# Attention for one query per head: the second halving moved to the last two quarters of a tile, and the norms read behind the third product

## The chip, the core and the metric

The kernel runs on one core of a Trainium2 chip. The metric is the device time of one execution in microseconds, lower is better. A ratio is the mean time of one kernel's fast runs over the mean of the other's fast runs in the same rounds, so it is not quite the ratio of the medians that are quoted. A difference counts as faster or slower when it is clear of 2% ("class" in the table of the experiments). Where two runs that differ by less are still called faster or slower than each other, the ranges of their single times don't overlap.

PE is the matrix engine, VectorE (DVE), ScalarE (ACT) and SyncE (SP) are the others used here; SP's queue issues the loads, ScalarE's the outputs. K(t) and V(t) are the loads of the keys and values of tile t. The norm is the sum by which an output is divided. A hole is a stretch in which fewer than half of the 16 DMA engines are at work.

## The reference

Eight batches of 32 heads, one query per head, 4096 keys and values of 128 numbers, all bf16:

```python
B, H, Sq, Skv, Dh = 8, 32, 1, 4096, 128
scale = q.shape[-1] ** -0.5
scores = jnp.einsum('bhqd,bhkd->bhqk', q, k) * scale
attn = _softmax(scores, axis=-1)
return jnp.einsum('bhqk,bhkd->bhqd', attn, v)
```

Each K and V is used once, so 537 MB have to come in and next to nothing goes out.

## The kernel before

The 256 heads go in 32 tiles of 8. A tile of K and a tile of V are 8.389 MB each (64 KB on each of 128 partitions), and three such buffers go round for both. For each tile, VectorE multiplies K by q quarter by quarter and halves the 128 products of a key to 64 (and in some quarters to 32); PE adds these up in groups with an identity matrix, 8 matmuls for 64 columns, 4 for 32; VectorE reduces what PE leaves.

```python
def width_of(t, u):
    return D // 4 if u < NU // 2 and t < NT - 3 else D // 2

def product(t, lo, hi):            # one quarter
    ...                            # tensor_tensor kt * qb, then first halving to D/2
    if width_of(t, c0 // UC) < D // 2:
        nc.vector.tensor_tensor(...)      # second halving to D/4

def sum_over_d(t, u):
    n = width_of(t, u) // DS              # DS = 8: 8 matmuls, or 4
    for s in range(n):
        nc.tensor.matmul(ps[:], lhsT=ident[:], rhs=kt[...], ...)
```

The values are multiplied in a loop on PE, one tile behind. The loop is a critical section (a block with a branch into it, which PE alone runs), and loads are kept behind it in program order:

```python
def values_loop(t):
    ...
    with tc.tile_critical() as loop:
        ...                                # 2 matmuls, 10 iterations of 6, 2 matmuls
    loops.append(loop)
```

Every two tiles, a norm is ready, and every eight tiles a finished block of 16 KB is sent out by ScalarE's queue:

```python
def finish_of(n):
    s, u = divmod(n, OB)                   # OB = 4
    ...
    nc.scalar.activation(out=stages[s][:, u, :], in_=ops.pop(n)[:], func=ACT.Copy, scale=rzs.pop(n)[:, 0:1])
    ...
    if u == OB - 1 or ...:
        nc.scalar.dma_start(o_n[s, ...], stages[s][...])

for t in range(NT):
    ...
    product(t, 0, Q)
    sum_over_d(t, 0)
    if t > 2 and t % R == 1:
        recip_of(n)
        finish_of(n)
    if t + 1 < NT:
        q_prep(t + 1)
    product(t, Q, 2 * Q)
    sum_over_d(t, 1)
    scores_of(t, 0)
    product(t, 2 * Q, 3 * Q)
    sum_over_d(t, 2)
    scores_of(t, 1)
    product(t, 3 * Q, C)
    sum_over_d(t, 3)
    scores_of(t, 2)
    if loop:
        values_loop(t - 1)
        load("k", t + 1)
        load("v", t)
    ...
```

## Time and profile before

| | before |
|---|---|
| time, median (lowest to highest) | 1300.55 us (1299.94 to 1301.36) |
| span of the profiled run | 1297.3 us |
| V issues apart, odd and even tiles, mean | 43.3 and 37.2 us |
| holes in the load stream | one of 5.1 us, 14 of 1.0 to 2.8 us |

Two groups of the page matter. A line gives the source line, the engine, the operation with its tiles and shapes, then busy time and mean, then the idle time ahead of these instructions and what ended most of it:

```profile
L217 DVE TENSOR_REDUCE sc<-ps 128x64 f32<-128x512 f32 x128 | 87.9, 687 | 116.2 <-PE ps L205 116.2
...
L336 DVE RECIPROCAL rz<-zp 16x1 f32<-16x1 f32 x16 | 2.5, 155 | 70.0 <-PE zp L328 70.0
```

VectorE (DVE) waits 116 us in all for PE's sums, most of it once at each tile's end, and 70 us, 4.7 on average in 15 odd tiles, for a norm that PE makes behind its loop.

### The profile page before, as it was taken

The numbers are of one execution on the slowest core, as the hardware profiler recorded it, in microseconds if no ns is written. First come the engines' busy times: TensorE is split into PE (matmuls) and PEld (weight loads), VectorE is DVE, ScalarE is ACT, GpSimd is POOL, SyncE is SP. The second block draws the span as 40 slices with busy tenths as digits, with TensorE's granted clock in tenths as the row PEclk, the third lists the DMA queues.
The fourth block names the chain that finished last, engine by engine and source line by source line (L and its number), as shares of the span: only waits on it lengthen the run. The fifth ranks groups of instructions, "written<-read, shape, count | busy, mean of one in ns | idle before, by whom it ended". The sixth has DMA issues, their size and how long they took to land. (4 is left out here: it accounts for less than half of the span.)

```text
span 1297.3 us, 11039 instructions
## 1 busy us (share of the span) xinstructions
PE 814.7 (63%) x3067; PEld 293.8 (23%) x3067; DVE 1040.1 (80%) x588; ACT 172.3 (13%) x625; POOL 3.3 (0%) x18
## 2 busy tenths in 40 slices
PE   1266576665776646776466764667646676567855
PEld 0022122221222212222122221222212222122212
DVE  5887886877969779687796878978788787887784
ACT  0111011110111101111011110111111111101111
POOL 0000000000000000000000000000000000000000
PEclk9998688786888868878688777887768887688867
DMA  9989999999999999999999999999999999999997
GB/s 422 420 356 443 429 390 451 390 420 421 420 421 409 430 390 421 451 390 421 421 420 421 396 445 388 436 437 386 422 388 451 423 388 451 390 420 434 403 451 300
DMA packets 11433, 537.33 MB, mean 414 GB/s; under 512 B 1808, under 2 KB 2064, under 8 KB 2320
## 3 DMA queue, kind: packets, MB, share of 16 engines
q1 hardware_dynamic: 11072, 536.94, 96.6%
q8 instruction: 14, 0.23, 0.1%
q10 hardware_dynamic: 336, 0.07, 0.0%
q14 instruction: 11, 0.09, 0.0%
HBM read 536.94 MB, written 0.07 MB: 414 GB/s over the span
## 5 line engine op out<-in xcount | busy, mean ns | idle before, releaser
L185 DVE TENSOR_TENSOR kt<-kt,qb 128x8192 bf16<-128x8192 bf16 x128 | 565.2, 4416 | 50.2 <-DMA kt<-in_k_dram 33.9
L205 PE MATMUL ps<-kt,ident 128*128 128x512 bf16 x792 | 316.0, 563 | 397.6 <-DVE kt L188 301.6
L288 PE MATMUL av<-vt,w 128*32 x1740 | 423.1, 382 | 9.8
L188 DVE TENSOR_TENSOR kt<-kt 128x4096 bf16<-128x4096 bf16 x128 | 293.4, 2292 | 4.4
L205 PEld LDWEIGHTS <-ident 128*128 128x128 bf16 x792 | 98.9, 129 | 596.9 <-issue 579.5
L288 PEld LDWEIGHTS av<-vt,w 128*32 x1740 | 165.4, 95 | 270.2 <-issue 146.3
L249 ACT ACTIVATE w<-sc,bias 128x256 bf16<-128x256 f32 x256 | 126.4, 494 | 711.1 <-DVE bias L240 711.1
L217 DVE TENSOR_REDUCE sc<-ps 128x64 f32<-128x512 f32 x128 | 87.9, 687 | 116.2 <-PE ps L205 116.2
L193 DVE TENSOR_TENSOR kt<-kt 128x2048 bf16<-128x2048 bf16 x58 | 71.0, 1225 | 2.0
L344 ACT ACTIVATE comb<-av 32x512 bf16<-32x512 f32 (+1 forms) x32 | 18.7, 586 | 322.7 <-PEq L278 316.7
L336 DVE RECIPROCAL rz<-zp 16x1 f32<-16x1 f32 x16 | 2.5, 155 | 70.0 <-PE zp L328 70.0
L274 PE MATMUL av<-vt,w 128*32 128x512 bf16 x116 | 42.0, 450 | 14.3 <-issue 12.7
L249 ACT ACTIVATION_READ_ACCUMULATOR w<-sc,bias 128x1 f32 x256 | 47.7, 186 | 0.0
L360 PE MATMUL op<-comb,pick 32*16 32x128 bf16 (+1 forms) x128 | 12.1, 213 | 25.6 <-ACT comb L344 25.6
L274 PEld LDWEIGHTS av<-vt,w 128*32 128x32 bf16 x116 | 6.8, 99 | 54.0 <-issue 54.0
L168 ACT ACTIVATE qg<-qh 8x128 bf16<-8x128 f32 x32 | 8.5, 266 | 69.1 <-PE qh L164 63.0
L170 PE MATMUL qp<-qg,heads 8*128 8x128 bf16 x32 | 7.0, 217 | 16.7 <-ACT qg L168 16.7
L360 PEld LDWEIGHTS <-pick 32*16 32x16 bf16 (+1 forms) x128 | 8.8, 83 | 32.7 <-issue 32.2
L164 PE MATMUL qh<-q_all,ident 128*8 128x128 bf16 x32 | 7.2, 224 | 13.1 <-DMA q_all<-in_q_dram 13.1
L229 DVE TENSOR_REDUCE pmax<-sc 128x1 f32<-128x256 f32 x32 | 13.4, 420 | 1.1
L316 PE MATMUL av<-vt,w 128*32 128x512 bf16 x191 | 14.0, 402 | 0.0
L172 ACT ACTIVATE qb<-qp 128x128 bf16<-128x128 f32 x32 | 8.9, 277 | 9.7 <-PE qp L170 9.7
(29 smaller groups left out, 50.7 us busy)
## 6 DMA issues: line engine op xcount, KB each, us to landing
kt<-in_k_dram SPq DMA_DIRECT2D x7, 4096.0 KB, 21.1
kt<-in_k_dram SPq DMA_DIRECT2D x2, 2048.0 KB, 14.0
vt<-in_v_dram SPq DMA_DIRECT2D x1, 4096.0 KB, 30.4
vt<-in_v_dram SPq DMA_DIRECT2D x1, 2048.0 KB, 34.9
vt<-in_v_dram SPq DMA_DIRECT2D x1, 1024.0 KB, 36.9
vt<-in_v_dram SPq DMA_DIRECT2D x1, 512.0 KB, 37.6
vt<-in_v_dram SPq DMA_DIRECT2D x31, 23.9
kt<-in_k_dram SPq DMA_DIRECT2D x28, 26.5
```

Of the source, the lines that this page charges most:

```text
L185: nc.vector.tensor_tensor(out=part, in0=part, in1=qb[:].to_broadcast([P, MC, D]), op=ALU.mult)
L188: nc.vector.tensor_tensor(out=part[:, :, 0 : D // 2], in0=part[:, :, 0 : D // 2], in1=part[:, :, D // 2 : D], op=ALU.add,)
L193: nc.vector.tensor_tensor(out=part[:, :, 0 : D // 4], in0=part[:, :, 0 : D // 4], in1=part[:, :, D // 4 : D // 2], op=ALU.add,)
L205: nc.tensor.matmul(ps[:], lhsT=ident[:], rhs=kt[:, u * UC : (u + 1) * UC, s * DS : (s + 1) * DS], start=(s == 0), stop=(s == n - 1),)
L217: made = nc.vector.tensor_reduce(out=scs[t][:, u * UC : (u + 1) * UC], in_=sums.pop((t, u))[:], axis=AX.X, op=ALU.add)
L229: nc.vector.tensor_reduce(out=pmax[:], in_=sc[:], axis=AX.X, op=ALU.max)
L249: nc.scalar.activation(out=w[:, :, g, :], in_=sc_g, func=ACT.Exp, bias=bias[:, g : g + 1], scale=scale, accum_out=esum[:, t % R, g : g + 1],)
L274: pe.matmul(av, lhsT=wf[:, i * nw : (i + 1) * nw], rhs=vf[:, i * nv : (i + 1) * nv], **how)
L288: pe.matmul(av, lhsT=wf[:, bass.ds(ow + i * nw, nw)], rhs=vf[:, bass.ds(ov + i * nv, nv)], start=False, stop=False,)
L316: nc.tensor.matmul(avs[t][j * AG : (j + 1) * AG, :], lhsT=w[:, i, :, :], rhs=vt[:, c0 : c0 + CB, :], start=(i < TG), stop=(j not in group[ ...
L344: nc.scalar.activation(out=comb[0:n, :, :], in_=av[0:n, :, :], func=ACT.Copy)
L360: nc.tensor.matmul(ops[n][:], lhsT=pick[0:e, m, r, :], rhs=comb[0:e, m, :], start=(r == 0 and m == 0), stop=(r == R - 1 and m == CB - 1),)
```

## The change

Its intent is to shorten what stands between the landing of a K tile and the release of its buffer. Four sums instead of eight remain at the end of a tile, and VectorE no longer stops for the norm in the middle of it.

```diff
-        return D // 4 if u < NU // 2 and t < NT - 3 else D // 2
+        return D // 4 if u >= NU // 2 and t < NT - 3 else D // 2
@@ the loop over tiles
             product(t, 0, Q)
             sum_over_d(t, 0)
-            if t > 2 and t % R == 1:
-                recip_of(n)
-                finish_of(n)
             if t + 1 < NT:
                 q_prep(t + 1)
             product(t, Q, 2 * Q)
@@
             sum_over_d(t, 2)
             scores_of(t, 1)
+            if t > 2 and t % R == 1:
+                recip_of(n)
+                finish_of(n)
             product(t, 3 * Q, C)
```

## The prediction

> **What bounds the kernel now.** I first read the page for the whole, then the queue that issues the loads, then a table of four tiles, then the timeline of the two VectorE stretches between them.
>
> ```profile
> DMA  9989999999999999999999999999999999999997
> q1 hardware_dynamic: 11072, 536.94, 96.6%
> HBM read 536.94 MB, written 0.07 MB: 414 GB/s over the span
> ```
>
> The kernel streams 537 MB and the DMA engines look full. But 414 GB/s is a mean over the span; what matters is what the stream does when nothing holds it. The table of stretches (length, then busy times by engine, granted clock, DMA share, GB/s) says it:
>
> ```profile
> 645.90:647.70 1.80, 1.37 (x5) 0.17 (x3) 0.96 (x2) 0.00 (x0) 0.00 (x0) 0.62 0.44 146
> 655.00:720.00 65.00, 41.09 (x151) 14.79 (x151) 53.15 (x29) 6.66 (x23) 0.00 (x0) 0.78 1.01 435
> ```
>
> Undisturbed it moves 435 GB/s, a load of 8.389 MB in 19.3 us; at 646 there is a hole. From the packets' starts and ends I counted such holes (fewer than half of the 16 engines at work): one of 5.1 us at 80, then 14, one every second tile (163.8, 243.5, 324.0 ... 1209.4), 1.0 to 2.8 us each and 30 us together. The issuing queue shows why:
>
> ```profile
> 603.34 0.33 SPq L151 DMA_DIRECT2D vt<-in_v_dram  x1
> 620.21 0.33 SPq L151 DMA_DIRECT2D kt<-in_k_dram  x1
> 646.70 0.33 SPq L151 DMA_DIRECT2D vt<-in_v_dram  x1
> 663.52 0.33 SPq L151 DMA_DIRECT2D kt<-in_k_dram  x1
> 683.87 0.33 SPq L151 DMA_DIRECT2D vt<-in_v_dram  x1
> 700.80 0.33 SPq L151 DMA_DIRECT2D kt<-in_k_dram  x1
> 727.29 0.33 SPq L151 DMA_DIRECT2D vt<-in_v_dram  x1
> ```
>
> Three buffers of a whole tile go round, so V(t) may be loaded when the last sum over K(t) on PE has ended, and K(t+2) when the loop over V(t-1) has (16.8 us after). V issues are 43.4 and 37.2 us apart in turn, 80.5 a pair. In the short (even) tile VectorE never waits for data. In the long (odd) one it waits for K, and the queue, already empty, waits for it:
>
> ```profile
> 609.16 4.42 DVE L185 TENSOR_TENSOR kt<-kt,qb 128x8192 bf16<-128x8192 bf16 x1 [3.88 <-DMA kt<-in_k_dram]
> ...
> 620.47 0.16 DVE L336 RECIPROCAL rz<-zp 16x1 f32<-16x1 f32 x1 [3.29 <-PE zp L328]
> ...
> 646.71 0.69 DVE L217 TENSOR_REDUCE sc<-ps 128x64 f32<-128x512 f32 x1 [3.06 <-PE ps L205]
> ```
>
> K lands at 609.2, V is issued at 646.7: 37.5 us, plus about 1 us to the first packet, while the two loads queued behind K take 2 x 19.3 = 38.6 us plus their own start. The hole is that chain, and 3.3 us of it is VectorE waiting for a norm behind the loop on PE, 3.1 us the eight last sums.
>
> **What the Trainium skill says.** "DMA: Bandwidth & Descriptors", Where 436 GB/s comes from: a fabric ceiling of 435.2 GB/s. The 435 above agrees, so the stream can't get faster; only holes can be closed. "TensorE: Matmul & The Clock Gate", Part 1: with 512 columns matmuls start 426.7 ns apart on a cold array and 215.7 ns warm, in windows of about 3.4 us. The trace agrees: eight sums take 3.57 us cold, 1.90 us right after the loop. So where the eight stand matters. "VectorE: DVE Perf Modes", Side-by-side: 2048 bf16 results of a tensor_tensor in 2x mode take about 1224 ns; the second halving measures 1225. "Perfetto Trace Analysis", Optimization Strategy: a gap that repeats on the engine that should be saturated can mean too few buffers; here it is the three.
>
> **The change part by part.** No instruction is added or removed: 58 second halvings and 792 sum matmuls remain, they change places. Rows used:
>
> ```profile
> 628.58 1.86 PE L205 MATMUL ps<-kt,ident 128*128 128x512 bf16 x4 [5.60 <-DVE kt L193]
> 643.10 3.57 PE L205 MATMUL ps<-kt,ident 128*128 128x512 bf16 x8 [3.69 <-DVE kt L188]
> 664.53 1.04 PE L205 MATMUL ps<-kt,ident 128*128 128x512 bf16 x4
> 1227.24 1.90 PE L205 MATMUL ps<-kt,ident 128*128 128x512 bf16 x8
> 1229.18 0.69 DVE L217 TENSOR_REDUCE sc<-ps 128x64 f32<-128x512 f32 x1 [4.49 <-PE ps L205]
> ```
>
> (a) The last quarter has 4 sums, not 8: cold, 3.57 becomes 1.86. V is issued 1.71 us sooner in every tile up to 28.
> (b) The first quarter has 8 warm sums behind the loop: 1.04 becomes 1.90, +0.86.
> (c) Each of the last two quarters has a second halving on VectorE, +1.27 each (from the first halving to the next instruction 2.21 becomes 2.33 + 1.15); each of the first two has 1.27 less.
> (d) The reciprocal no longer stands between the first two quarters. Its norm is finished by the third, so it costs about 0.1 and waits for nothing.
>
> Two recurrences result. *From K's landing* (if K is late): 2 x 6.7 for the first two quarters, then 0.60 + 4.45 + 2.33 + 1.15 = 8.53 each for the last two, 0.13 to PE, 1.86 of sums: 13.4 + 17.1 + 2.0 = 32.5 us, against 37.5 now. That is 5 us sooner, more than the 2.2 us hole. *From V issue to V issue over PE*: loop, copy, output sums, first quarter's 8 sums, their reduction. Tile 30 of the kernel before, which has no second halvings, already has this form: V issue 1209.39, reduction at 1229.18, so 19.8 us. Then 2 x 8.53 + 0.13 + 1.86 + 0.03: 38.9 us. Before it was 18.9 + 2 x 7.26 + 0.13 + 3.57 = 37.2, as seen. So the even tile gets 1.7 us *longer* and the odd one falls to the same 38.9. VectorE reaches its first reduction about 15.4 us after V issue, PE 19.8, so VectorE now waits there some 4.4 us in every tile. And K may land some 4 us late without harm.
>
> The DMA needs 38.6 us per tile. One engine of the 16 falls about 1.2 us behind whenever one of the 14 instruction packets of 16 KB (page part 3, queue q8, about one in 98 us) comes by; at worst, always on the same engine, this adds 0.5 a tile: 38.6 to 39.1. So both limits lie at 38.9 to 39.1, against 80.5 / 2 = 40.2. I take 39.1 for steps that don't always mesh.
>
> The sum: tiles 0 and 1 are VectorE's, without a loop in front, and lose 1.71 each: V(1) at 84.3 - 3.4 = 80.9 (a hole of about 1.7 us stays there). 27 tiles of 39.1 bring V(28) to 1136.6. Tile 29 (no second halvings, before and after) takes about 38.3: V(29) at 1174.9, before 1209.4. From there to the end, 87.9 us, nothing changes. That is 34.5 us less. 1300.6 - 34.5 = 1266; for waits I haven't seen I add 2: **1268 us, 2.5% less**.
>
> **Rivals.** *1. The PE chain becomes longer than I say.* The loop used to begin behind eight sums that had nearly warmed the array; now it begins 1.7 us sooner in the clock's window and runs its first 1 to 4 us cold. For: cold matmuls come 427 ns apart, while the loop issues one in 251. Against: loops that began up to 2.0 us before the clock rose (tile at 969.5) still ended 16.86 us after V issue, against 16.82 for others, because six warm matmuls need 1.3 us of the 1.5 us an iteration takes, and the queue catches up. If it costs 0.6 us a tile, 16 us of the gain go: 1284. *2. DMA was full anyway* (96.6%), so only bits come back. For: the page. Against: the holes, 35 us in all, and 435 GB/s between them. If half of the holes reopen elsewhere (K late, the slow engine lagging ever further): 1284 as well. *3. Only the odd tile matters and the even one keeps 37.2.* Then DMA's 38.6 sets the pace and no more: 1254 to 1258. Against: the wait of 4.49 us at 1229.18, which shows the even tile can't. *4. Slower*: would need over 41 us a tile; nothing shows that.
>
> **Range and chances.** Every 0.1 us per tile is 2.7 us in the end. 38.85 gives about 1260, 39.5 about 1277. Two per cent less is 1274.6, or 39.4 us per tile: above my estimate of either limit, but only by 0.3. So faster by over 2% 0.74, within 2% 0.25, slower 0.01; range 1261 to 1278.
>
> **What would show it right or wrong.** Right: V issues about 39 us apart without alternation; the holes at every second tile gone and a mean of some 425 GB/s; no wait of VectorE for the norm; a wait of 4 to 5 us for the first quarter's sums in every tile up to 28; the wait at the tile's end near 1.4 us instead of 3.1; VectorE's waits for K short or gone. Wrong: an interval from V to K well above 17 us (rival 1); V issues even but 39.5 or more apart with VectorE waiting for K (rival 2); alternation still there.

## The result

| | before | after |
|---|---|---|
| time, median (lowest to highest) | 1300.55 us (1299.94 to 1301.36) | 1280.87 us (1280.28 to 1282.37) |
| ratio, 95% interval | | 0.985, 0.9833 to 0.9867: the same at 2% |
| span of the profiled run | 1297.3 us | 1280.6 us |

The kernel is 1.5% faster. The prediction was 1268 us with a range up to 1278, and faster by over 2% at 0.74. The measured time lies 13 us above the one and 3 us above the other.

The load stream of the changed kernel, from its page:

```profile
q1 hardware_dynamic: 11072, 536.94, 98.0%
HBM read 536.94 MB, written 0.07 MB: 419 GB/s over the span
```

It is fuller than the 96.6% and 414 GB/s of before, but below the 425 GB/s that the prediction named as the sign of success. In one tile of it, VectorE's timeline (start, duration, line, operation, and in brackets the idle time before and what ended it) is mostly as foretold:

```profile
616.99 0.69 DVE L217 TENSOR_REDUCE sc<-ps 128x64 f32<-128x512 f32 x1 [2.07 <-PE ps L205]
...
626.12 0.15 DVE L336 RECIPROCAL rz<-zp 16x1 f32<-16x1 f32 x1
...
636.13 0.69 DVE L217 TENSOR_REDUCE sc<-ps 128x64 f32<-128x512 f32 x1 [1.35 <-PE ps L205]
...
640.20 4.42 DVE L185 TENSOR_TENSOR kt<-kt,qb 128x8192 bf16<-128x8192 bf16 x1 [2.14 <-DMA kt<-in_k_dram]
```

The reciprocal waits for nothing, the wait at the tile's end is 1.35 us instead of 3.06, there is a new wait for the first quarter's sums, and K is waited for in odd and even tiles alike. What was not foretold is in the queue that issues the loads:

```profile
353.62 0.33 SPq L151 DMA_DIRECT2D vt<-in_v_dram  x1
370.44 0.33 SPq L151 DMA_DIRECT2D kt<-in_k_dram  x1
392.53 0.33 SPq L151 DMA_DIRECT2D vt<-in_v_dram  x1
419.36 0.33 SPq L151 DMA_DIRECT2D kt<-in_k_dram  x1
441.32 0.33 SPq L151 DMA_DIRECT2D vt<-in_v_dram  x1
```

As a rule V issues are 38.9 us apart, and K follows V after 16.8 us. But here K follows after 26.8 and the next V after 48.8. Of the 28 intervals from V(1) to V(29) three are like that: 48.8, 43.7 and 44.4 us. Against 38.9 these are 20.2 us too much in all. They belong to tiles 9, 17 and 25. The timeline of PE and of ScalarE's queue in tile 9 shows what happened:

```profile
383.10 7.00 ACTq L375 DMA_DIRECT2D out_dram<-stage  x1
...
390.63 1.86 PE L205 MATMUL ps<-kt,ident 128*128 128x512 bf16 x4 [6.71 <-DVE kt L193]
...
402.75 1.03 PE L274 MATMUL av<-vt,w 128*32 128x512 bf16 x2 [10.25 <-DMA out_dram<-stage]
```

The last sums end at 392.5. The loop over the values (L274 is its first line) should begin 0.4 us later, and it begins 10.2 us later, when an output transfer has landed. The load stream then runs dry. This is the view of stretches of the changed kernel, in the order length, busy times, granted clock, DMA share, GB/s:

```profile
415.00:420.30 5.30, 4.40 (x22) 1.64 (x20) 0.00 (x0) 0.59 (x1) 0.00 (x0) 1.00 0.00 0
```

In the kernel before, the same transfer of the same tile was issued at 380.54, and its loop was not late:

```profile
380.54 5.98 ACTq L375 DMA_DIRECT2D out_dram<-stage  x1
...
405.82 0.61 PE L274 MATMUL av<-vt,w 128*32 128x512 bf16 x2 [0.55 <-issue]
```

There the transfer had 25 us until the loop; now it has 10. The last packets of the three outputs end at 401.6, 718.1 and 1035.3 in the changed kernel, and the three late loops begin at 402.75, 719.04 and 1036.06, 0.8 to 1.2 us later each time:

```profile
719.04 1.04 PE L274 MATMUL av<-vt,w 128*32 128x512 bf16 x2 [5.06 <-DMA kt<-in_k_dram]
...
1036.06 1.03 PE L274 MATMUL av<-vt,w 128*32 128x512 bf16 x2 [5.54 <-DMA out_dram<-stage]
```

(For the second the profile names a load of K as the releaser; that load landed at 718.78, the output at 718.58, so the label alone decides nothing. In both_send_loop below, the same loop begins at 704.44, well before that K, on which VectorE starts at 709.86.)

### The profile page after: what moved, and what is told of

Read it like the earlier page. It is cut to its first block, busy times and chain, and to the rows that moved or that the text cites. A ratio compares the mean times of both kernels' runs of the same rounds, so it can differ in the third digit from the quotient of the medians.

```text
span 1280.6 us, 11028 instructions
## 1 busy us (share of the span) xinstructions
PE 766.2 (60%) x3067; PEld 287.8 (22%) x3067; DVE 1040.6 (81%) x588; ACT 172.4 (13%) x625; POOL 3.3 (0%) x18
## 5 line engine op out<-in xcount | busy, mean ns | idle before, releaser
L185 DVE TENSOR_TENSOR kt<-kt,qb 128x8192 bf16<-128x8192 bf16 x128 | 565.2, 4416 | 70.0 <-DMA kt<-in_k_dram 58.5
L205 PE MATMUL ps<-kt,ident 128*128 128x512 bf16 x792 | 261.0, 480 | 419.9 <-DVE kt L193 369.7
L288 PEld LDWEIGHTS av<-vt,w 128*32 x1740 | 173.0, 99 | 263.9 <-issue 123.2
L205 PEld LDWEIGHTS <-ident 128*128 128x128 bf16 x792 | 84.5, 113 | 571.2 <-issue 523.2
L274 PE MATMUL av<-vt,w 128*32 128x512 bf16 x116 | 47.3, 501 | 34.0 <-DMA out_dram<-stage 15.8
L274 PEld LDWEIGHTS av<-vt,w 128*32 128x32 bf16 x116 | 7.1, 101 | 74.1 <-issue 73.7
L369 ACT ACTIVATE stage<-op,rz 16x128 bf16<-16x128 f32 x16 | 5.7, 358 | 132.4 <-DVE rz L336 132.0
L316 PE MATMUL av<-vt,w 128*32 128x512 bf16 x191 | 15.4, 418 | 0.0
## 6 DMA issues: line engine op xcount, KB each, us to landing
vt<-in_v_dram SPq DMA_DIRECT2D x1, 1024.0 KB, 38.7
```

The costliest lines, as they stand in the source:

```text
L185: nc.vector.tensor_tensor(out=part, in0=part, in1=qb[:].to_broadcast([P, MC, D]), op=ALU.mult)
L205: nc.tensor.matmul(ps[:], lhsT=ident[:], rhs=kt[:, u * UC : (u + 1) * UC, s * DS : (s + 1) * DS], start=(s == 0), stop=(s == n - 1),)
L274: pe.matmul(av, lhsT=wf[:, i * nw : (i + 1) * nw], rhs=vf[:, i * nv : (i + 1) * nv], **how)
L288: pe.matmul(av, lhsT=wf[:, bass.ds(ow + i * nw, nw)], rhs=vf[:, bass.ds(ov + i * nv, nv)], start=False, stop=False,)
L316: nc.tensor.matmul(avs[t][j * AG : (j + 1) * AG, :], lhsT=w[:, i, :, :], rhs=vt[:, c0 : c0 + CB, :], start=(i < TG), stop=(j not in group[ ...
```

## The experiments

Theory A: the loop's entry waits for every transfer issued ahead of it, so the moved output stalls it three times, and that is where the missing gain went. Theory B: the load stream was full anyway, or the stalls have another cause that only coincides with the output. Beside it stood the question which of the two parts carries the gain. Eleven kernels ran, three rounds each; all gave correct results.

| run | median us | median before | ratio | 95% interval | class |
|---|---|---|---|---|---|
| both_send_behind | 1281.81 | 1299.55 | 0.9855 | 0.9839 to 0.9872 | same |
| widths_only | 1316.61 | 1299.55 | 1.0132 | 1.0115 to 1.0149 | same |
| norms_only | 1276.19 | 1299.55 | 0.9815 | 0.9799 to 0.9832 | unclear |
| norms_send_behind | 1275.20 | 1299.55 | 0.981 | 0.9794 to 0.9827 | unclear |
| both_send_loop | 1260.92 | 1299.74 | 0.9701 | 0.9685 to 0.9717 | faster |
| norms_send_loop | 1264.34 | 1299.74 | 0.9724 | 0.9708 to 0.974 | faster |
| norms_second | 1265.50 | 1299.74 | 0.9726 | 0.971 to 0.9742 | faster |
| before_send_late | 1301.29 | 1299.74 | 1.001 | 0.9994 to 1.0027 | same |
| after_sends_doubled | 1273.43 | 1299.71 | 0.9798 | 0.9781 to 0.9814 | unclear |
| both_norm_second | 1264.47 | 1299.71 | 0.9724 | 0.9708 to 0.974 | faster |
| first_last_send_loop | 1255.81 | 1299.71 | 0.9661 | 0.9645 to 0.9677 | faster |

### both_send_behind: the output behind the loop, which did not get there

```diff
+    def send_of(n):                 # the dma_start, taken out of finish_of
...
             if loop:
                 values_loop(t - 1)
                 load("k", t + 1)
                 load("v", t)
+            if t > 2 and t % R == 1:
+                send_of(n)
```

> The changed kernel, only with the three 16 KB output transfers standing behind the loop over the values in program order (same engine, issued at the same moment, still behind the third product), so that the loop's entry no longer waits for them. Theory A (the loop's entry stalls 10.0, 4.6 and 5.1 us for these transfers, and that is where the missing gain went): V issues 38.9 to 39.1 us apart throughout, loop entries 0.4 us after V issue in all 29 tiles, time about 1264 us, 1261 to 1268. Theory B (the load stream is full anyway and its packets slow down, the stalls are hidden behind it): 1276 to 1281, hardly faster than the changed kernel's 1280.9.

It took 1281.81 us, and the stalls were all there. Taken alone this speaks for theory B:

```profile
403.34 1.03 PE L274 MATMUL av<-vt,w 128*32 128x512 bf16 x2 [11.00 <-DMA out_dram<-stage]
```

But the list of ScalarE's instructions as compiled showed that the edit had not done what it was meant to do. The output transfer still stood in front of the branch into the critical section:

```
(ScalarE, order as compiled, waits left out)
L369 Activation stage<-op,rz 16x128
L378 DMACopy out_dram<-stage 16x4x128
L458 UnconditionalBranch
L249 Activation w,esum<-sc,bias 128x64x4
```

A place in the source behind the loop is not enough. The loads of K and V are held behind it by an explicit dependence, and the output had none. So this run does not tell the two theories apart. The same list shows, on PE, that in front of the branch into the critical section stand waits on ScalarE, VectorE, GpSimd and every DMA semaphore in use.

### widths_only: the first part alone

```diff
-        return D // 4 if u < NU // 2 and t < NT - 3 else D // 2
+        return D // 4 if u >= NU // 2 and t < NT - 3 else D // 2
```

> Only the second halving moves to the last two quarters; the norm is read between the first two quarters as before. By the chain over PE: the even tile 38.9 us; in the odd tile VectorE waits for the norm until 17.1 us after V issue, then 6.7 us for the second quarter and 19.1 us to the next V issue, 42.9 us. A pair is 81.8 us against 80.5 before, so about 1315 us, 1308 to 1320: slower than before. No stall at loop entries, since the outputs are issued early. If instead the shorter tail (1.7 us a tile) is a gain by itself, it comes to about 1276.

It took 1316.61 us, 1.3% slower than before. V issues are 42.9 and 38.9 us apart in turn (610.42, 653.33 and 692.15 for example), as the two chains say. VectorE in an odd tile:

```profile
614.34 4.43 DVE L185 TENSOR_TENSOR kt<-kt,qb 128x8192 bf16<-128x8192 bf16 x1 [1.98 <-DMA kt<-in_k_dram]
...
627.54 0.15 DVE L336 RECIPROCAL rz<-zp 16x1 f32<-16x1 f32 x1 [6.45 <-PE zp L328]
```

The first quarter has lost its second halving, so VectorE comes to the norm sooner and waits for it longer, 6.45 us here. The time taken out in front of that wait is lost, and the time put in behind it is paid. A shorter tail is no gain by itself here.

### norms_only: the second part alone

The move of `recip_of` and `finish_of` as in the change, with the halvings on the first two quarters as before.

> Only reciprocal, scaling and output move behind the third product; the halvings stay on the first two quarters. The chain from K's landing to V issue falls from 37.5 to 34.2 us and the one over PE stays 37.2 us, both below what the load stream needs (39.1 us a tile in the changed kernel's first eight tiles), so the holes close without the widths' move. The three stalls at the loop's entry stay (4 to 10 us each) but more of them is hidden since the chain over PE has 2 us to spare each tile: 1265 to 1276 us. If the widths' move carries the gain, this is above 1285.

It took 1276.19 us, just above the expected 1265 to 1276, and faster than the whole change. The stalls are there in the same three tiles:

```profile
406.27 1.04 PE L274 MATMUL av<-vt,w 128*32 128x512 bf16 x2 [10.15 <-DMA out_dram<-stage]
```

The intervals from V to K are 26.96, 21.39 and 21.41 us instead of 16.8, 19.3 us too much in all. But only the first left a hole in the stream (5.0 us at 419). This kernel's chain over PE takes 37.2 us a tile and so can make up part of a delay afterwards; in the changed kernel it takes 38.9 us and can't.

### norms_send_behind

norms_only with the edit of both_send_behind.

> norms_only with the output transfers behind the loop as in both_send_behind. Theory A and a load stream of 39.1 us a tile: 1262 to 1267 us, within 3 us of both_send_behind, because the load stream sets the pace in both and the widths' move is worth nothing any more. If the widths' move has a worth of its own, this is over 5 us slower than both_send_behind.

It took 1275.20 us, as norms_only, for the same reason: the output was still ahead of the branch. It tells nothing more.

### both_send_loop: the output really behind the loop

```diff
-            nc.scalar.dma_start(o_n[s, ...], stages[s][...])
+            behind_loop(nc.scalar.dma_start(o_n[s, ...], stages[s][...]))
```

> both_send_behind as it was meant: there the scheduler had still placed the output transfer ahead of the branch into the loop (the order of ACT's instructions shows it) and the stalls stayed (out packets end at 402.2, 719.2, 1036.5, loops start at 403.3, 720.2, 1037.2). Now a dependence keeps the transfer behind that branch; nothing else differs from the changed kernel. Theory A (the loop's entry waits for every transfer issued ahead of it): all loops start 0.4 us after V issue (0.4 to 0.6), the holes at 415, 440, 757, 1053, 1074 (11.6 us together) are gone, and the load stream alone sets the pace at 39.1 to 39.3 us a tile: 1264 to 1270 us. Theory B (the coincidence of transfer and stall has another cause, instruction fetch say): stalls stay, 1279 to 1283.

It took 1260.92 us, 3.0% faster than before and 3 us below the expected range. The timeline of tile 9:

```profile
382.90 6.35 ACTq L378 DMA_DIRECT2D out_dram<-stage  x1
...
392.34 0.33 SPq L151 DMA_DIRECT2D vt<-in_v_dram  x1
...
392.87 1.04 PE L274 MATMUL av<-vt,w 128*32 128x512 bf16 x2 [0.56 <-issue]
```

The transfer is issued at the same moment as in the changed kernel (382.90 against 383.10), and its packets move at the same time, from 392.6 to 401.2. The loop begins at 392.87, just after the first of them. All late loops and all later holes are gone. So it is not the transfer that costs, in bandwidth or otherwise, but the wait for it at the loop's entry. Theory A holds and B falls.

### norms_send_loop

The same for norms_only.

> The same for norms_only (halvings on the first two quarters as before). Its only holes were 4.9 us at 80 and 5.0 us at 419, the latter behind the first stall, so 5 us less than its 1276.2: 1269 to 1273 us. Without stalls the widths' move is then worth only the smaller first hole (1.7 against 4.9 us), so about 3 us slower than both_send_loop; if the load stream is not the limit, more.

It took 1264.34 us, 5 us better than expected, and 3.4 us slower than both_send_loop, as expected. With no stalls left, that is what the widths' move is worth, and it is about the difference in the first hole, at 80: 5.1 us here against 1.9.

### norms_second: the norm behind the second product

```diff
             scores_of(t, 0)
+            if t > 2 and t % R == 1:
+                recip_of(n)
+                finish_of(n)
             product(t, 2 * Q, 3 * Q)
```

> The kernel before with reciprocal, scaling and output behind the second product instead of between the first two: no change to the widths, no special place for the output. The norm is ready there (17 us after V issue, VectorE arrives at 19), so no wait of VectorE; the output is issued some 8 us earlier than in norms_only and lands (14 to 19 us) at or before the loop's entry. Expected 1269 to 1274 us, as norms_send_loop, with the three loop entries late by under 2 us. If theory B holds and the stalls have nothing to do with the output, 1275 to 1277 as norms_only.

It took 1265.50 us, 3.5 below the expected range. The first late loop is still late, by 4.9 us (V at 394.28, loop at 399.59), which missed the expected 2; the other two are not. So a transfer that is issued one product sooner lands in time in two of the three tiles, without any special place in the order.

### before_send_late: nothing moved

`send_of` behind the third product in the kernel before, norms and scaling left in place.

> The kernel before with the output transfer alone moved behind the third product; norms, scaling and halvings as before. Theory A: three stalls appear that the kernel before does not have, about 8, 4 and 4 us, each followed by holes in the load stream, so 5 to 15 us slower than the kernel before. Theory B: no change, within 2 us.

It took 1301.29 us, the same as before, against 5 to 15 us expected. The profile shows why this is no evidence for theory B:

```profile
381.61 4.67 ACTq L378 DMA_DIRECT2D out_dram<-stage  x1
```

The transfer went out at 381.6, 1.1 us later than before. ScalarE does not wait for VectorE's products; behind the scaling it only had two small copies in the way. The experiment did not delay what it was meant to delay.

### after_sends_doubled: more outputs, each half as large

```diff
-OB = 4
+OB = 2
```

> The changed kernel with an output transfer after every second pair instead of every fourth (8 KB each instead of 16), so that seven of them, not three, are issued behind a third product with a loop to follow. Nothing else changes. Theory A: seven late loop entries, the first by some 10 us, the others by about 5, against 10.0, 4.6 and 5.1: some 20 us more delay of the V issues, of which a part is hidden: 1291 to 1303 us. If the stalls depend on bytes rather than on the presence of a transfer, each is halved and the total stays near 1281.

It took 1273.43 us: faster than the changed kernel, against 1291 to 1303 expected. There are six late entries (the seventh output lands in time), but each is late by only 1.9 to 2.5 us, 13.3 in all. The expectation had the number of stalls nearly right and their size wrong; the other outcome it named, stalls halved with the bytes and a total near 1281, is closer, but not right either. The changed kernel's output, then this one's, in the view of the issuing line:

```profile
DMA to landing us min/median/max: 1.4/14.0/19.0
```

```profile
DMA to landing us min/median/max: 1.3/10.9/11.6
```

These medians include the short outputs at the end. In front of late loops the six of 8 KB landed after 10.8 to 11.6 us, the three of 16 KB after 19.0, 14.0 and 14.6. What counts is the landing less the 9.8 us from issue to the loop's normal entry (383.10 and 392.93 in tile 9 of the changed kernel), so 3 us less of landing halve the delay. The first output's 19.0 us contain an issue of 7.00 us; here no issue takes over 0.39. What makes that one slow stays open; it is slow in the kernel before too (5.98).

### both_norm_second

The move of norms_second in the changed kernel.

> The changed kernel with reciprocal, scaling and output behind the second product instead of the third, and no special place for the output. The transfer is issued some 8.5 us earlier, about 18 us before V issue, and lands after 14 (the first after 19): by theory A the second and third stall are gone and the first is 1 to 5 us: 1261 to 1267 us. Without theory A: 1279 to 1283.

It took 1264.47 us, inside the expected range, with one late entry (20.36 us from V to K instead of 16.82).

With this the stalls can be added up. Take both_send_loop as the kernel without them, and add to its 1260.9 us what the intervals from V to K have above 16.82:

| kernel | late entries, sum | 1260.9 + sum | measured |
|---|---|---|---|
| both_norm_second | 3.5 | 1264.4 | 1264.5 |
| after_sends_doubled | 13.3 | 1274.2 | 1273.4 |
| the changed kernel | 20.6 | 1281.5 | 1280.9 |
| both_send_behind | 22.4 | 1283.3 | 1281.8 |

Within 1.5 us each microsecond of stall is a microsecond of time in these four. With the shorter chain of norms_only it is less: 19.3 us of stall cost it 11.9 (1276.2 against the 1264.3 of norms_send_loop).

### first_last_send_loop: what sets the pace then

```diff
-        return D // 4 if u >= NU // 2 and t < NT - 3 else D // 2
+        return D // 4 if u in (0, NU - 1) and t < NT - 3 else D // 2
```

on top of both_send_loop: four sums behind the loop and four at the end.

> both_send_loop with the second halving on the first and the last quarter of a tile: 4 sums right behind the loop and 4 at the end, so the chain over PE is 18.9 + 7.3 + 8.5 + 2.0 = 36.8 us a tile instead of 38.9. If that chain is what still sets the pace in both_send_loop (38.93 us a tile), this gains up to 1.5 us a tile, below 1250 us. If the load stream is the limit as well (norms_send_loop, with a chain of 37.2 us and no holes, took 38.95 us a tile), nothing is gained: 1258 to 1263 us.

It took 1255.81 us, 3.4% faster than before, between the two expectations. V issues are 38.71 us apart on average (V(1) at 80.93, V(29) at 1164.76, 28 tiles), against 38.90 in both_send_loop over the same 28. Its page:

```profile
q1 hardware_dynamic: 11072, 536.94, 99.3%
HBM read 536.94 MB, written 0.07 MB: 428 GB/s over the span
```

VectorE's waits agree: those for PE's sums fell from 105.1 to 59.2 us in all, those for K rose from 72.6 to 103.3. So the chain over PE was most likely the pace of both_send_loop, with the load stream's own limit only 0.2 us a tile below it. At 38.7 us a tile, two loads of 19.35, with one hole of 1.1 us, the load stream is the limit. Why norms_send_loop, whose chain takes 37.2 us, needed 38.95 us a tile is not settled by these runs.

## Why the prediction was wrong

**What held.** The bound, the holes and their cause were read rightly. (a) The last sums became 1.86 us. (b) and (c) The chain over PE was put at 38.9 us; undelayed tiles measure 38.9 and the 27 tiles of both_send_loop 38.93. V(1) was put at 80.9 and came at 80.99. The even tile did get longer and the odd one fell to the same length. V issues no longer alternate. Three of the signs failed: 419 GB/s instead of 425, the wait for the first quarter's sums (below), and VectorE's waits for K, which were to be short or gone and rose from 33.9 us in all (12 times) to 58.5 (23 times).

**The step that failed is (d)**: the reciprocal "costs about 0.1 and waits for nothing". That is true of the reciprocal and was taken for the whole part. With it move the scaling and, in tiles 9, 17 and 25, the output transfer, from 25 us ahead of the loop to about 10. The transfer needs 14 to 19 us to land, and the loop's entry waits for it. The prediction asked what waits in front of the moved instructions and not who waits behind them. A delay of 0 was put down where 20.2 us of V issues were lost.

**The sum.** 17.8 us lie between the predicted span, 1262.8, and the measured one, 1280.6. They are the 20.2 of the stalls; less 3.8, because I took 39.1 us a tile where the chain's own 38.9 (38.96 as the mean of 27 tiles with the stalls taken off) was right; and 1.6 more behind V(29), 89.5 us instead of 87.9. Why the end takes 1.6 longer was not looked into. The 2 us added "for waits I haven't seen" were a tenth of what was needed; the conversions of the range (38.85 to 1260, 39.5 to 1277) leave them out. Without the stalls the kernel takes 1260.9, just below the predicted range: then the estimate erred by 7 us the other way, mostly through the 39.1 where 38.93 was right, 4.5 us in 27 tiles, and the 2 us. The 435 GB/s were a little generous as well: that row has a DMA share of 1.01, since packets count where they start, and the fastest stream of any run here, two loads in 38.7 us, is 433.

**Rivals.** *1* (a cold array at the loop's start) is not what happened. Loops of both_send_loop began up to 4.2 us before the clock rose and still let K go 16.82 us after V. The intervals from V to K did grow, though, the sign that the prediction gave for this rival, and for another reason. *2* (the stream is full anyway) had about the right size, 1284, and the wrong cause: with the stalls gone it runs at 427 GB/s. *3* was refuted as argued. The wait for the first quarter's sums was put at 4.4 us and measures 2.1 to 2.3 in the tiles from 597 to 675 (0.5 to 4.8 in others without a late loop), because K now lands about 4 us after V issue there and VectorE spends the other 2 us waiting for that.

**The parts.** Only without the stalls is the whole better than each of its parts. The widths alone make the kernel 1.3% slower, since the time saved vanishes in the wait for the norm. The norms alone give more than the whole change did. Added to them, the widths' move costs 4.7 us where the outputs stall the loop (1280.9 against 1276.2) and gives 3.4 where they don't (1260.9 against 1264.3).

## What to carry to other kernels

When a group of instructions is moved later, follow every one of them to its last consumer, those with no apparent consumer too: a store that nobody reads can still be waited for at the next barrier, loop entry or critical section. Look at how much time each moved transfer had until then, and measure how long a small store takes to land when the engines are full of large loads. And look at the compiled order before trusting an experiment: two of these eleven moved a line of source and left the transfer ahead of the loop, and a third hardly moved it in time.

## What the Trainium skill lacked or had wrong

- No page gives the time that a small store needs among large loads. "DMA: Bandwidth & Descriptors", Queues, rings and completion order, says that each DMA engine takes turns between the queue rows at packet granularity. The trace agrees for the second and third output of the changed kernel: their 256-byte packets come in series 2.43 us apart (708.02, 710.44, 712.87, 715.30), the time of a 64 KB packet of the loads, 2.42 us. Most packets of the first came closer together. What follows from it is not on the page: 16 KB landed after 14.0 and 14.6 us (19.0 for the first, with its slow issue), 8 KB after 10.8 to 11.6.
- No page that I read says that a branch into a critical section on one engine waits for all transfers issued ahead of it. In this program such waits stand in the compiled list, and they cost 10.0, 5.0 and 5.6 us from V to K.
- "DMA: Bandwidth & Descriptors", Where 436 GB/s comes from, says that for loads from HBM the HBM side (about 358 GB/s) binds, without a condition, though its own measurement of one core, with the other core of the pair idle, is 425. Here the measurement decides: with one core running, first_last_send_loop reached 428 GB/s over a whole execution.
- No page that I read has it that a cold start of PE can cost nothing: in both_send_loop the loop, which issues a matmul every 252 ns on average, ran for up to 4.2 us at half the clock and still ended 16.82 us after V issue.
